# A decode block with a key and value cache: the load buffers moved by 192 bytes in SBUF

## The chip, the cores and the metric

The kernel runs on one core of a Trainium2 chip. The core has a matrix engine (TensorE, PE in the profile), a vector engine (VectorE, DVE), an activation engine (ScalarE, ACT), a general engine (GpSimd, POOL) and a sync engine (SyncE, SP) that issues transfers here. Transfers between the device memory and the on-chip memory (SBUF, 128 partitions) run on 16 transfer engines. SBUF is addressed by partition and by byte within the partition; this case is about the byte at which buffers begin. The metric is the device time of one execution in microseconds.

## The reference

The input `x` has 4 rows of 512. It is normalized to mean 0 and variance 1 over the 512 and goes into two branches, whose results are added to `x`:

```python
xn = layernorm(x)                                   # (4, 1, 512)
q  = (xn @ wq)                                      # 4 batches x 32 heads x 128
s  = einsum("bhqd,bhkd->bhqk", q, k_cache) * 128**-0.5   # over 4096 positions
o  = einsum("bhqk,bhkd->bhqd", softmax(s), v_cache)
out = x + o_flat @ wo + silu(xn @ w1) @ w2
```

`k_cache` and `v_cache` are 4 batches x 32 heads x 4096 positions x 128 floats each, 268 MB apiece; `wq` and `wo` are 8.4 MB each, `w1` and `w2` (512 x 1792 and back) 3.7 MB each. Everything is float32. There is one query per batch and head, so each element of the caches is used once.

## The kernel before

A tile of the cache holds four heads of one batch: 4 x 4096 positions x 128 floats, put on 128 partitions with 128 positions of 128 floats each. That is 65536 bytes a partition, contiguous in the device memory as well as in SBUF, and 8.389 MB in all. There are T = 32 such tiles of K and 32 of V, and the main loop (line 338) runs over them.

SBUF is given out by pools (lines 68 to 71), in this order: `const` for constants, `kpool` with two buffers of a tile, `vpool` with one, and `small` for short-lived tiles. So the size of all the tiles in `const` sets the byte at which the first buffer of `kpool` begins, and the following ones come right behind. A tile is asked for with a shape, a type and a name; nothing is executed by that.

All large transfers are issued by SyncE, in the order of the program: `load_tile` (line 76) asks for a buffer and issues one transfer, at line 80. The buffers also serve for other things: `w1` and `x` are loaded into parts of a K buffer (lines 84 to 91), `wq` into the V buffer (line 92), and at the end `wo` into the V buffer and `w2` into a K buffer, cut into pieces (lines 363 to 370). A transfer waits on SyncE until its buffer is free.

In step i of the loop:

- SyncE issues the K tile of step i + 1 and then, when the value matmuls of step i - 1 have let go of the single V buffer, the V tile of step i.
- `products` (line 265) multiplies K by the query on VectorE, 32 positions of each partition at a time, in place; the query comes from PSUM. GpSimd (line 269) adds the upper half of the 128 products to the lower half, for some of the positions, and VectorE sums what is left (`sums`, lines 280 and 281).
- `maxima` (lines 285 to 293) takes the maximum over four rows of partitions, `softmax` (line 299) exponentiates on ScalarE into `p_t`.
- `values` (line 310) multiplies `p_t` by V on TensorE: 32 instructions in the program, 64 matmuls in the trace, into the PSUM tile `o_ps`.
- `heads_out` (lines 323 to 331) sorts the four heads out and adds them into the PSUM tile `o_all`.

The last V tile goes into a K buffer (line 352). After the loop the heads are divided by their sums, transposed and multiplied by `wo` and most of `w2` (line 404), the rest of `w2` is added by `accumulate` (line 148), and the result goes out through `res` (lines 413 to 417).

Of the kernel before, what the change touches and what calls it, by code (L numbers as in the profile page):

```python
# [8 lines left out]
F32 = mybir.dt.float32  # L9
# [14 lines left out]
def kernel(  # L24
# [24 lines left out]
    P = nc.NUM_PARTITIONS  # L49
# [18 lines left out]
    const = ctx.enter_context(tc.tile_pool(name="const", bufs=1))  # L68
# [7 lines left out]
    def load_tile(pool, name, cache, i):  # L76
        t = pool.tile([P, R, Dh], F32, name=name)
        h, b = i // B * G, i % B
        src = cache[b, h : h + G].rearrange("h s d -> (h s) d")
        nc.sync.dma_start(t, src.rearrange("(p r) d -> p r d", p=P))  # L80
        return t
# [11 lines left out]
    nc.sync.dma_start(wq_t, wq.rearrange("(p c) n -> p c n", p=P))  # L93
    ks = {0: load_tile(kpool, "k_t", k_cache, 0)}

    ident = const.tile([P, P], F32, name="ident")
    make_identity(nc, ident)
    ones = const.tile([P, 1], F32, name="ones")
# [351 lines left out]
```

## Time and profile before

| | us |
|---|---|
| median of 3 runs | 1308.52 (1308.26 to 1309.41) |
| the profiled execution | 1307.8 |
| its span, first to last instruction | 1306.0 |
| VectorE busy | 973.8 (75%) |
| GpSimd busy | 510.9 (39%) |
| TensorE busy | 354.7 (27%) |
| ScalarE busy | 92.6 (7%) |
| read from the device memory | 561.00 MB, 430 GB/s over the span |

Times in the profile are microseconds unless marked ns, L12 is line 12 of the kernel, and "out<-in" names the tiles that an instruction writes and reads. A strip of 40 digits divides the span (or a stretch of it) into equal slices; a digit is the busy share in tenths. Rows of the transfer queues give the packets, their bytes, and the time that they took as a share of the time of 16 engines; the smallest packets carry a few bytes, the largest one partition of a load. In the rows by stretch, the pairs are busy time and number of instructions of TensorE, its weight loads, VectorE, ScalarE and GpSimd, and behind them come the granted clock of TensorE, the share of the transfer engines and the rate in GB/s. A row of waits reads: engine, what waited, what it waited for, then the total in us, how many times, and the longest.

### The profile page before, as it was taken

The page shows a single profiled execution, that of the slowest core. Times are in us where ns is not written, and L with a number is a line of the kernel's source. Part 1 is how long each engine was busy: PE and PEld are TensorE (multiplying, and loading weights), DVE is VectorE, ACT ScalarE, POOL GpSimd, SP SyncE. Part 2 cuts the span into 40 slices and gives each one's busy share as a digit, 9 for nine tenths or more (in the row PEclk, how much of TensorE's full clock was granted, in tenths as well). Part 3 has the DMA queues.
Part 4 walks back from the last instruction along what each step waited for, and adds up shares of the span by engine and source line. Part 5 has one row for each costly group of instructions (what it writes and reads, how often), then busy time and mean ns, then how long its engine had stood idle before and what let it go on. Part 6 is the DMA issues. An engine that isn't in the chain of part 4 may idle for free.

```text
span 1306.0 us, 6301 instructions
## 1 busy us (share of the span) xinstructions
PE 354.7 (27%) x2484; PEld 87.0 (7%) x2484; DVE 973.8 (75%) x540; ACT 92.6 (7%) x297; POOL 510.9 (39%) x142
## 2 busy tenths in 40 slices
PE   4221223221223321133322132322122232113237
PEld 1000000000000000000000000000000000000002
DVE  1499777887777797777797777788777789777770
ACT  1010000000000000000000000000000000000000
POOL 0255333444333444332444433344433344433340
PEclk9755666656666665666665566665566666566668
DMA  9999999999999999999999999999999999999997
GB/s 408 442 426 442 424 440 428 438 430 438 430 434 434 432 436 430 438 428 438 430 432 436 432 434 432 434 432 436 430 436 430 438 428 440 426 442 422 444 420 330
DMA packets 10437, 561.40 MB, mean 430 GB/s; under 512 B 1172, under 2 KB 1188, under 8 KB 1448
## 3 DMA queue, kind: packets, MB, share of 16 engines
q1 hardware_dynamic: 10392, 561.01, 99.4%
q8 instruction: 19, 0.31, 0.1%
q14 instruction: 10, 0.08, 0.0%
q10 hardware_dynamic: 16, 0.00, 0.0%
HBM read 561.00 MB, written 0.01 MB: 430 GB/s over the span
## 4 chain that ended last, share of the span: by engine, by line
DMA 70%; PE 22%; another core or an unknown queue 4%; DVE 2%; issue 2%; POOL 0%; ACT 0%; SPq 0%; POOLq 0%; ACTq 0%
DMA v_t<-in_A_v_cache_dram 61%; PE o_ps L310 20%; DMA k_t<-in_A_k_cache_dram 4%; DMA k_t<-in_A_v_cache_dram 3%; DMA v_t<-in_A_wq_dram 2%; DVE k_t L265 1%; PE q_ps L404 1%; PE sm L219 1%; DVE s L281 1%; POOL k_t L269 0%; DVE s L280 0%; PE acc L148 0%; PE sm L391 0%; PE q_ps L233 0%
## 5 line engine op out<-in xcount | busy, mean ns | idle before, releaser
L269 POOL TENSOR_TENSOR k_t<-k_t 128x2048 f32<-128x2048 f32 (+1 forms) x128 | 508.6, 3985 | 748.5 <-DVE k_t L265 748.5
L265 DVE TENSOR_TENSOR k_t<-k_t,q_ps 128x4096 f32<-128x4096 f32 x128 | 562.3, 4414 | 226.9 <-DMA k_t<-in_A_k_cache_dram 226.9
L310 PE MATMUL o_ps<-v_t,p_t 128*16 128x512 f32 x1984 | 285.2, 739 | 829.8 <-DMA v_t<-in_A_v_cache_dram 829.8
L281 DVE TENSOR_REDUCE s<-k_t 128x32 f32<-128x2048 f32 (+1 forms) x128 | 257.7, 2014 | 11.9 <-POOL k_t L269 11.9
L310 PEld LDWEIGHTS o_ps<-v_t,p_t 128*16 128x16 f32 x1984 | 66.5, 113 | 1030.1 <-issue 951.1
L323 ACT ACTIVATE o_sb<-o_ps 128x512 f32<-128x512 f32 x32 | 19.1, 597 | 1097.8 <-issue 1081.9
L280 DVE TENSOR_REDUCE s<-k_t 128x16 f32<-128x2048 f32 x32 | 72.8, 2276 | 0.0
L299 ACT ACTIVATE p_t<-s,nb 32x128 f32<-32x128 f32 x128 | 66.5, 519 | 17.4 <-DVE nb L293 14.0
L326 DVE TENSOR_TENSOR o_sb<-o_sb,own 128x512 f32<-128x512 f32 x32 | 21.7, 678 | 26.5 <-ACT o_sb L323 26.4
L331 PE MATMUL o_all<-o,w_t 128*32 128x128 f32 x64 | 15.7, 336 | 88.7 <-DVE o L330 88.7
L330 DVE TENSOR_REDUCE o<-o_sb 128x128 f32<-128x512 f32 x32 | 32.8, 1024 | 3.2
L299 ACT ACTIVATION_READ_ACCUMULATOR p_t<-s,nb 32x1 f32 x128 | 25.5, 199 | 0.0
L331 PEld LDWEIGHTS o_all<-o,w_t 128*32 128x32 f32 x64 | 4.9, 118 | 118.0 <-DVE o L330 118.0
L414 DVE COPY s<-acc 128x128 f32<-128x128 f32 x1 | 0.3, 292 | 14.8 <-PE acc L148 14.8
L310 PE MATMUL o_ps<-k_t,p_t 128*16 128x512 f32 x64 | 8.4, 684 | 6.5 <-DMA k_t<-in_A_v_cache_dram 6.5
L404 PE MATMUL q_ps<-v_t,ot 128*4 128x512 f32 x64 | 9.9, 788 | 0.4 <-DVE ot L396 0.4
L285 DVE TENSOR_REDUCE m_t<-s 128x1 f32<-128x128 f32 x32 | 9.1, 285 | 1.1
L208 DVE COPY ht_sb<-sm 128x64 f32<-128x64 f32 x1 | 0.2, 224 | 12.7 <-PE sm L201 12.7
L293 DVE STREAM_TRANSPOSE nb<-mb 128x32 f32<-128x32 f32 x32 | 6.8, 212 | 3.3
L219 PE MATMUL sm<-v_t,xpad 128*32 128x512 f32 x64 | 8.5, 690 | 1.3 <-DMA v_t<-in_A_wq_dram 1.3
L250 PE MATMUL q_ps<-q_h,ident 32*32 32x512 f32 x64 | 8.5, 599 | 0.8 <-DVE q_h L240 0.8
L229 DVE COPY o_sb<-sm 128x512 f32<-128x512 f32 x1 | 0.7, 692 | 9.5 <-PE sm L219 9.5
(74 smaller groups left out, 72.0 us busy)
## 6 DMA issues: line engine op xcount, KB each, us to landing
v_t<-in_A_wo_dram SPq DMA_DIRECT2D x2, 4096.0 KB
k_t<-in_B_w_dram SPq DMA_DIRECT2D x1, 3584.0 KB, 11.3
k_t<-in_B_w_dram SPq DMA_DIRECT2D x1, 1792.0 KB, 31.9
k_t<-in_B_w_dram SPq DMA_DIRECT2D x1, 1024.0 KB, 34.0
k_t<-in_A_k_cache_dram SPq DMA_DIRECT2D x32, 48.5
k_t<-in_B_w_dram SPq DMA_DIRECT2D x1, 512.0 KB, 34.8
v_t<-in_A_v_cache_dram SPq DMA_DIRECT2D x31, 29.3
k_t<-in_B_w_dram SPq DMA_DIRECT2D x1, 256.0 KB, 35.0
```

What stands on the lines that cost most here:

```text
L219: nc.tensor.matmul(qp[32 * j : 32 * j + 32, :], xpad[:, c, a : a + PH], wq_t[:, c, n * G * Dh : (n + 1) * G * Dh], start=(m == 0 and c == ...
L265: nc.vector.tensor_tensor(k[:, a:z, :], k[:, a:z, :], q[:, None, :].to_broadcast([P, STEP, Dh]), op=ALU.mult)
L269: nc.gpsimd.tensor_tensor(k[:, a:v, :half], k[:, a:v, :half], k[:, a:v, half:], op=ALU.add)
L280: nc.vector.tensor_reduce(s[:, v:z], k[:, v:z, :], axis=AX, op=ALU.add)
L281: nc.vector.tensor_reduce(s[:, a:v], k[:, a:v, :half], axis=AX, op=ALU.add)
L299: nc.scalar.activation(p_t[rows, :, g], s[rows, :], AF.Exp, bias=nb[rows, :1], scale=scale, accum_out=l_t[rows, i % B, i // B, g : g + 1],)
L310: last = nc.tensor.matmul(o[j : j + NR * G, :], p_t[:, rows, :].rearrange("p r g -> p (r g)"), v[:, rows, :].rearrange("p r d -> p (r d)") ...
L323: nc.scalar.activation(o_sb.rearrange("p r d -> p (r d)"), o_ps, AF.Copy)
L326: nc.vector.tensor_tensor(o_sb, o_sb, own[:, :, None].to_broadcast([P, NR, Dh]), op=ALU.mult)
L330: nc.vector.tensor_reduce(o_1, o_sb.rearrange("p r d -> p d r"), axis=AX, op=ALU.add)
L331: nc.tensor.matmul(o_all[:, b, :], w_t[:, W0 - h : W0 - h + H], o_1, start=False, stop=(i == T - 1))
L404: nc.tensor.matmul(part[j : j + B, :], a, w, start=(c < 4), stop=(c >= len(rows) - 4))
```

## The change

One tile is added to the pool `const`, after `xpad` and ahead of `ident`:

```diff
     ks = {0: load_tile(kpool, "k_t", k_cache, 0)}
 
+
+    const.tile([P, 48], F32, name="fill")
     ident = const.tile([P, P], F32, name="ident")
```

It has 48 floats, 192 bytes, on each partition. No instruction writes or reads it. The tiles of `const` behind it and all the buffers of `kpool`, `vpool` and `small` begin 192 bytes further on; the buffers of the loads begin at byte 26880, which is 105 x 256. All other lines are the same, and those behind the added ones have numbers larger by 2.

## The prediction

> **What bounds the kernel now.** I read the two strips of the page for the transfers first, then the chain of waits, then single steps of the loop, then the packets of the transfer queue.
>
> ```profile
> span 1306.0 us, 6301 instructions
> DVE  1499777887777797777797777788777789777770
> DMA  9999999999999999999999999999999999999997
> DMA packets 10437, 561.40 MB, mean 430 GB/s; under 512 B 1172, under 2 KB 1188, under 8 KB 1448
> ```
>
> The transfer engines are busy in every slice but the last, while VectorE, the busiest compute engine, sits at seven or eight tenths. The chain of waits in order of time shows how one step of the loop hangs on them (start, duration, what):
>
> ```profile
> 1060.39 9.48 PE o_ps L310 x64
> 1069.90 29.06 DMA v_t<-in_A_v_cache_dram
> 1098.96 0.14 issue
> 1099.09 8.91 PE o_ps L310 x64
> 1108.02 29.64 DMA v_t<-in_A_v_cache_dram
> 1137.66 0.14 issue
> 1137.79 10.04 PE o_ps L310 x64
> ```
>
> The value matmuls of two neighbouring steps start 1099.09 - 1060.39 = 38.70 us and 1137.79 - 1099.09 = 38.70 us apart. The step is therefore not set by matmuls, whose bursts vary from 8.91 to 10.04 us. The busy time in those two steps, by engine, with the share of the transfer engines and their rate at the end of each row:
>
> ```profile
> 1060.39:1099.09 38.70, 10.84 (x74) 2.49 (x75) 30.20 (x17) 2.68 (x9) 15.89 (x5) 0.63 1.00 432
> 1099.09:1137.79 38.70, 9.28 (x66) 2.26 (x67) 30.41 (x18) 2.68 (x9) 15.88 (x5) 0.63 1.00 434
> ```
>
> VectorE (third pair) works 30.2 to 30.4 us of 38.70, TensorE 9 to 11, GpSimd 15.9; the transfer share is 1.00. A step loads one K tile and one V tile, 2 x 8.389 MB. So the kernel is a transfer stream at 16.78 MB / 38.70 us = 433.5 GB/s, with compute beside it. Who waits tells how much cover the compute has:
>
> ```profile
> PE o_ps L310 <- DMA v_t<-in_A_v_cache_dram: 829.8, 31, 46.8
> DVE k_t L265 <- DMA k_t<-in_A_k_cache_dram: 226.9, 30, 9.2
> ```
>
> TensorE waits for every V tile. VectorE waits 226.9 / 30 = 7.6 us for a K tile. In the chain above a V load needs 29.06 to 29.64 us from issue to landing, of which its own share is half a step, 19.35; so it stands about 9.8 us behind a K load that is still moving, and the transfer engines are never without work.
>
> **The change, part by part.** It adds a tile and no instruction: no compute, no transfer, no wait, no step moved past a queue. It does three things.
>
> *The place of everything after it.* 48 floats are 192 bytes. The load buffers move from 26880 - 192 = 26688 bytes (104 x 256 + 64) to 26880 (105 x 256). A buffer is 65536 bytes a partition, also a multiple of 256, so all three had the same offset of 64 and all three lose it. Every constant after `xpad`, and the small tiles behind the buffers, move by the same 192, so the buffers, `p_t` and `q_h` keep their distances; `xpad` alone stays and is read only in the start-up.
>
> *The compute.* Whether an engine reads the shifted buffers at another speed no row tells. The present times on both K buffers are, as minimum, median and maximum:
>
> ```profile
> L265 DVE TENSOR_TENSOR k_t<-k_t,q_ps x128: 4394/4412/4422, 51.9 to 1253.2; 128x4096 f32<-128x4096 f32 x128
> ```
>
> VectorE can lose 38.70 - 30.3 = 8.4 us per step before it sets the pace, 28% of its work. TensorE can lose the 9.8 us by which the V load is issued ahead of its turn; that would double its burst. I cost the compute at 0 under this cover. If the cover went, the products of L265 would be late next.
>
> *The packets.* This is the only term that could matter. In the stretch of 26 steps, and in two short stretches at the end that hold nothing but small packets, the transfer queues show (packets, MB, share of 16 engines):
>
> ```profile
> DMA packets 7514, 436.83 MB, mean 433 GB/s; under 512 B 832, under 2 KB 832, under 8 KB 832
> q1 hardware_dynamic: 7493, 436.54, 100.1%
> ...
> DMA packets 2, 0.00 MB, mean 0 GB/s; under 512 B 2, under 2 KB 2, under 8 KB 2
> q1 hardware_dynamic: 2, 0.00, 0.2%
> ...
> DMA packets 32, 0.01 MB, mean 2 GB/s; under 512 B 16, under 2 KB 32, under 8 KB 32
> q10 hardware_dynamic: 16, 0.00, 0.5%
> q1 hardware_dynamic: 16, 0.00, 0.5%
> ```
>
> The first pair of rows is from 129.34 to 1137.79 us: 7493 - 832 = 6661 large packets carry 436.54 MB, 65536 bytes each, one for each partition of a load. Sixteen engines share the 256 of a step, so an engine moves 16 of them in 38.70 us, 2.419 us each. The second pair covers 0.5 us with two of the smallest packets: 0.2% of 16 x 0.5 us is 16 ns, 8 ns each, though they carry almost nothing. The third covers 3.5 us: 1.0% of 16 x 3.5 is 0.56 us; without 16 of the smallest at 8 ns it leaves 0.43 us for the 16 packets of the output, which are 8 KB in all, 512 bytes each: 27 ns each. At the stream's rate 512 bytes take 2419 x 512 / 65536 = 18.9 ns. So a packet has a fixed cost of about 8 ns; with the shares rounded to a tenth it is 4 to 12.
>
> How many packets count? The end follows the last V tile, here in a K buffer:
>
> ```profile
> 1274.14 8.39 PE L310 MATMUL o_ps<-k_t,p_t 128*16 128x512 f32 x64 [6.50 <-DMA k_t<-in_A_v_cache_dram]
> 1288.08 9.93 PE L404 MATMUL q_ps<-v_t,ot 128*4 128x512 f32 x64 [0.38 <-DVE ot L396]
> 1302.78 0.29 DVE L414 COPY s<-acc 128x128 f32<-128x128 f32 x1 [14.76 <-PE acc L148]
> ```
>
> From its landing to the last copy 28.6 us pass in matmuls and small operations that no alignment shortens, with the weights arriving beside them. Up to that landing an engine has moved 8 packets for each of 64 K and V loads, for `wq` and for `w1`: 66 x 8 = 528. The sum is therefore 528 times the change in one packet, and every ns per packet is 0.53 us. The queue being full, all of it reaches the end.
>
> What is that change? At the one end, the whole fixed cost is due to the offset and goes: -8 ns, -4.2 us (by the 12 ns, -6.3). At the other end, nothing excludes a loss; I bound it by the same cost coming twice, +4.2 us. Between them I go by the row that is nearest, the smallest packets: they write no load buffer and pay 8 ns all the same. The cost is then that of a packet, not of where a buffer begins. I take 0 ns. The sum is 0 on a span of 1306.0 us. The profiled execution took 1307.8 us in all, 0.7 below the median of 1308.52; with no change the forecast is that median, 1308.5.
>
> The Trainium skill, page "DMA: Bandwidth & Descriptors", section "Where 436 GB/s comes from", gives a ceiling of 435.2 GB/s. The trace's 433.5 agrees in being just below; by the page, an estimate, a step at the ceiling would be 38.55 us, and 33 such steps would save 5.0 us, so it too leaves no room for a large gain.
>
> **The rivals.**
>
> *A. The 64 bytes below the offset are moved and thrown away.* Each packet would then carry 65600 bytes' worth of time for 65536: 2419 x 64 / 65536 = 2.4 ns, times 528 = 1.25 us. Without it the time is 1307.3. For it speaks that 2.4 ns fits inside the 8 ns; against it, that the offset is on the written side while the caches are read from rows of 65536 bytes. That rule is in the same page of the Trainium skill, section "How a descriptor splits into AXI transactions": a transaction must start at a 256-byte boundary, and the bytes ahead of the start are fetched without use. The page tells it of reading, and no run here shows it yet for writing.
>
> *B. The fixed cost is the offset's.* A packet that begins and ends inside a 256-byte block may pay for two broken pieces instead of none. Then all 8 ns go: 1308.5 - 4.2 = 1304.3. For it: nothing in this kernel is loaded to another offset, so no row separates the two. Against it: the smallest packets' 8 ns, and the output's 8 ns, whose destination is not a load buffer.
>
> *C. Slower: packets that begin on the boundary get longer.* The place is the write of each 64 KB packet into the buffers; for instance, engines that now start on the same boundary could hold each other up. If the fixed cost doubles, 528 x 8 ns = 4.2 us, 1312.7. It decides from 0.2%, 2.6 us, that is 5 ns a packet. Against it: the buffers keep their distances to each other and all shared one offset before, too. For it: only that no row excludes it.
>
> *D. The change doesn't do what it says.* The tile is never written or read; if it got no room, nothing would move and the time would stay 1308.5. The time can't tell this from the forecast.
>
> **How the numbers follow.** The three times shown spread over 1308.26 to 1309.41, 0.09%, so I take 0.2%, 2.6 us, as what a measurement can tell from no change. Chances: forecast 0.40, A 0.25, B 0.17, C 0.15, D 0.03. The forecast, A and D lie within 0.2%: 0.68. B is faster, 0.17. C is slower, 0.15. The likeliest case's own range is 1306.9 to 1309.6 (A to the highest time shown, each with 0.03% of spread). The range for 8 in 10 takes in B at 1304.3 with some spread, and the smaller half of C: 1303.7 to 1311.0.
>
> **What would show each step.** If I am right, the steps of the loop stay at 38.70 us between value matmuls and the last V tile lands 1274 us after the start. By A they are 16 x 2.4 ns = 0.04 us shorter, by B 0.13 us (38.57), by C 0.13 us longer; the last landing moves by 1.25, 4.2 or -4.2 us. L265 should stay at 4.41 us and the bursts of L310 at 8.4 to 10 us; another time there would show that compute feels the offset, within its cover. The stretch from the last landing to the last copy should stay at 28.6 us. The prediction is wrong if a packet's time depends on the buffer's place by more than 5 ns, or if the offset changes what a transfer does for every piece of 256 bytes, of which a packet has 256: a single ns on each would be 256 ns a packet and 135 us in all. The stream's steadiness near one rate is my reason to think that this isn't so.

## The result and the profile after

The changed kernel takes 1305.28 us (median; 1304.97 to 1306.11) beside 1308.10 us (1307.72 to 1309.59) for the kernel before: the ratio is 0.9978, with a 95% interval of 0.9970 to 0.9986, so it is 1.8 to 3.9 us faster. That is 2.8 us, just beyond the 2.6 us that the prediction took as the bound of no change, and 3.2 us below the forecast of 1308.5. One execution of a later run, the one at offset 128, took 1670.35 us, far from the other 11, and is left out of its time and ratio. The profiled execution took 1305.64 us, 1303.9 of it span. Lines of the kernel behind the new tile have numbers larger by 2: L310 is L312, L265 is L267.

The strips of the page say what they said before:

```profile
span 1303.9 us, 6301 instructions
DVE  1499777887777797777797777788777779777770
DMA  9999999999999999999999999999999999999997
DMA packets 10437, 561.40 MB, mean 431 GB/s; under 512 B 1172, under 2 KB 1188, under 8 KB 1448
```

The same 10437 packets with the same bytes pass in 2.1 us less. The chain of waits over the same two steps, and the busy time in them:

```profile
1058.23 8.85 PE o_ps L312 x64
1067.09 29.63 DMA v_t<-in_A_v_cache_dram
1096.86 10.01 PE o_ps L312 x64
1106.88 28.49 DMA v_t<-in_A_v_cache_dram
1135.51 9.46 PE o_ps L312 x64
```

```profile
1058.23:1096.86 38.63, 10.20 (x75) 2.42 (x75) 30.09 (x17) 2.68 (x9) 15.91 (x5) 0.63 1.00 435
1096.86:1135.51 38.65, 10.50 (x67) 2.43 (x68) 30.55 (x18) 2.69 (x9) 15.90 (x5) 0.59 1.00 434
```

The two steps are 38.63 and 38.65 us long, not 38.70: 0.06 us less on average. An engine moves 16 large packets in a step, so a packet takes about 0.06 / 16 = 4 ns less. Two steps give the size only roughly: over 26 steps the mean fell from (1137.79 - 129.34) / 26 = 38.79 us to (1135.51 - 129.13) / 26 = 38.71, 0.08 us or 5 ns a packet. The transfer share is still 1.00; the same engines are full, with less to do. VectorE's product is as long as it was, and the waits for K and V hardly move:

```profile
L267 DVE TENSOR_TENSOR k_t<-k_t,q_ps x128: 4395/4413/4422, 51.5 to 1250.8; 128x4096 f32<-128x4096 f32 x128
...
PE o_ps L312 <- DMA v_t<-in_A_v_cache_dram: 826.2, 31, 46.5
...
DVE k_t L267 <- DMA k_t<-in_A_k_cache_dram: 224.6, 30, 9.0
```

The end, in order of time:

```profile
1271.72 9.57 PE L312 MATMUL o_ps<-k_t,p_t 128*16 128x512 f32 x64 [7.21 <-DMA k_t<-in_A_v_cache_dram]
...
1300.62 0.29 DVE L416 COPY s<-acc 128x128 f32<-128x128 f32 x1 [12.90 <-PE acc L150]
```

The last V tile lands at 1271.72 us, 2.42 us earlier than at 1274.14. From there to the last copy it is 28.90 us, 0.26 more than before; the burst of matmuls at the landing took 9.57 us here and 8.39 there, which is within what such bursts vary by. So the gain is made in the stream, and the tail passes it on.

### The profile page after: what moved, and what is told of

It reads as the page before. It is cut to its first block, busy times and chain, and to the rows that moved or that the text cites. A ratio compares the mean times of both kernels' runs of the same rounds, so it can differ in the third digit from the quotient of the medians.

```text
span 1303.9 us, 6301 instructions
## 1 busy us (share of the span) xinstructions
PE 356.0 (27%) x2484; PEld 88.1 (7%) x2484; DVE 973.8 (75%) x540; ACT 92.7 (7%) x297; POOL 511.2 (39%) x142
## 2 busy tenths in 40 slices
DMA packets 10437, 561.40 MB, mean 431 GB/s; under 512 B 1172, under 2 KB 1188, under 8 KB 1448
## 4 chain that ended last, share of the span: by engine, by line
DMA 71%; PE 23%; another core or an unknown queue 4%; issue 2%; DVE 0%; ACT 0%; SPq 0%; ACTq 0%
DMA v_t<-in_A_v_cache_dram 65%; PE o_ps L312 21%; DMA k_t<-in_A_v_cache_dram 3%; DMA v_t<-in_A_wq_dram 2%; PE q_ps L406 1%; PE sm L221 1%; PE sm L393 0%; PE acc L150 0%; PE q_ps L235 0%; PE q_ps L252 0%; DVE o L332 0%; DVE o_sb L328 0%; DVE q_h L242 0%; DVE o_sb L231 0%
## 5 line engine op out<-in xcount | busy, mean ns | idle before, releaser
L267 DVE TENSOR_TENSOR k_t<-k_t,q_ps 128x4096 f32<-128x4096 f32 x128 | 562.3, 4414 | 224.6 <-DMA k_t<-in_A_k_cache_dram 224.6
L312 PE MATMUL o_ps<-v_t,p_t 128*16 128x512 f32 x1984 | 286.1, 741 | 826.2 <-DMA v_t<-in_A_v_cache_dram 826.2
L312 PEld LDWEIGHTS o_ps<-v_t,p_t 128*16 128x16 f32 x1984 | 66.6, 113 | 1027.3 <-issue 948.3
L312 PE MATMUL o_ps<-k_t,p_t 128*16 128x512 f32 x64 | 9.6, 765 | 7.2 <-DMA k_t<-in_A_v_cache_dram 7.2
```

Source lines behind the costliest of these rows:

```text
L267: nc.vector.tensor_tensor(k[:, a:z, :], k[:, a:z, :], q[:, None, :].to_broadcast([P, STEP, Dh]), op=ALU.mult)
L312: last = nc.tensor.matmul(o[j : j + NR * G, :], p_t[:, rows, :].rearrange("p r g -> p (r g)"), v[:, rows, :].rearrange("p r d -> p (r d)") ...
```

## The experiments

By now the theory was that the offset of the buffers, their distance behind a multiple of 256 bytes, costs something in each packet. It had to be told from others: that some other tile's place matters, that the cost grows with the offset (the prediction's A), and that each packet pays a fixed price at any offset (its B). All kernels are the kernel before with the edits shown; their ratios are to the kernel before, run on the same chip.

**Moving everything by 256 bytes.**

```diff
+    const.tile([P, 64], F32, name="fill")
     ident = const.tile([P, P], F32, name="ident")
```

> The fill tile has 64 floats, 256 bytes: everything moves further than in the change, but the load buffers keep their offset of 64 bytes from a multiple of 256. If the offset is the cause, the time is that of the kernel before (1308.1 us, ratio 1.000) and a step of the loop stays at 38.70 us. If moving things in itself or another address is the cause, the time falls by about 2.8 us, to 1305.3.

Measured: 1308.02 us, ratio 0.9998 (0.9990 to 1.0007). The value matmuls of three steps start at 1060.52, 1099.22 and 1137.92 us, 38.70 us apart as expected. Other addresses with the same offset of 64 bytes give the time of the kernel before; moving alone does nothing that these runs can tell.

**Only the load buffers.**

```diff
     ot = const.tile([P, H, B], F32, name="ot")
+    const.tile([P, 48], F32, name="fill")
```

> The same 48 floats, but as the last tile of the constants: the load buffers and the small tiles move by 192 bytes to the multiple of 256, the constants (ident, p_t, q_h and the others) stay where they were. If the load buffers' offset is the cause, all of the gain is there: 1305.3 us, ratio 0.998, step of 38.62 us. If it is the constants that an engine reads, the time stays at 1308.1.

Measured: 1305.32 us, ratio 0.9980 (0.9972 to 0.9989): the whole gain, with the constants where they were before. What counts is the place of the buffers (or of the small tiles behind them, which move too; the next pairs, in which the packets are multiplied, rule these out).

**Other offsets.** The same tile with 16, 32 and 56 floats puts the buffers 128, 192 and 32 bytes behind a multiple of 256:

```diff
+    const.tile([P, 16], F32, name="fill")
     ident = const.tile([P, P], F32, name="ident")
```

> 16 floats: the load buffers begin 128 bytes behind a multiple of 256. If the bytes below the offset are moved and thrown away, the cost grows with the offset and is twice that of 64 bytes: some 2.8 us slower than the kernel before, 1310.9 (1309.4 by the strict price of 1.25 us per 64 bytes). If a broken piece at each end of a packet is the cause, any offset costs the same: 1308.1. If only multiples of 128 matter: 1305.3.

> 32 floats: the load buffers begin 192 bytes behind a multiple of 256. Bytes thrown away: three times the cost of 64 bytes, 5.6 us slower than the kernel before, 1313.7 (1310.6 by the strict price). A broken piece at each end: 1308.1 as before.

> 56 floats: the load buffers begin 32 bytes behind a multiple of 256. Bytes thrown away: half of the cost of 64 bytes, 1.4 us faster than the kernel before, 1306.7 us. A broken piece at each end: no change, 1308.1.

Measured, with 64 and 0 beside them (32 ran on another chip than 64, 128 and 192; there the kernel before took 1308.29 us, and 1308.05 with those):

| offset, bytes | us | ratio to before (95%) |
|---|---|---|
| 0 (the change) | 1305.28 | 0.9978 (0.9970 to 0.9986) |
| 32 | 1308.75 | 1.0003 (0.9994 to 1.0012) |
| 64 (moved by 256) | 1308.02 | 0.9998 (0.9990 to 1.0007) |
| 128 | 1307.80 | 0.9998 (0.9989 to 1.0006) |
| 192 | 1308.10 | 0.9999 (0.9990 to 1.0008) |

The bursts of value matmuls in the chains of waits, two following ones each at offset 128, then 192, then 32, then with the buffers alone moved to 0:

```profile
1099.09 8.41 PE o_ps L311 x64
1137.79 9.54 PE o_ps L311 x64
```

```profile
1099.17 9.05 PE o_ps L311 x64
1137.88 8.46 PE o_ps L311 x64
```

```profile
1099.41 8.87 PE o_ps L311 x64
1138.12 9.99 PE o_ps L311 x64
```

```profile
1097.23 8.70 PE o_ps L310 x64
1135.87 9.86 PE o_ps L310 x64
```

The steps are 38.70, 38.71 and 38.71 us at the three offsets and 38.64 at 0. Bytes thrown away in proportion to the offset would have put 192 bytes 2.5 us above the kernel before by the strict price; it is not there. A has fallen: 64, 128 and 192 bytes cost the same within the intervals. Whether 32 costs a little more stayed open here.

**Only V.** The tile of 48 floats goes first into the pool of V, so that K keeps the offset of 64:

```diff
+    vpool.tile([P, 48], F32, name="fill")
     wq_t = vpool.tile([P, R, Dh], F32, name="v_t")...
```

> 48 floats as the first tile of the pool of V: only the V buffer moves to a multiple of 256, both K buffers keep the offset of 64 bytes. If the cost lies in the packets, V's 33 of the 66 loads lose it: half of the gain, 1.4 us, 1306.7 us, and a step of 38.66 us. If it is only the K buffers, which VectorE and GpSimd read and write, 1308.1; if only V, 1305.3.

Measured: 1306.45 us, ratio 0.9987 (0.9978 to 0.9996), 1.8 us below the kernel before on that chip; the interval is 0.5 to 2.9 us. It takes in half of the gain and excludes no gain; the whole gain it does not exclude. The value matmuls of two following steps:

```profile
1059.11 9.64 PE o_ps L311 x64
1097.77 9.09 PE o_ps L311 x64
```

That step is the 38.66 us that was expected of half the packets. Over 26 steps, from 129.16 to 1136.41 us, the mean is 38.74, between the 38.79 of the kernel before and the 38.71 of the change. The small tiles behind the V buffer move here too, but the constants and the K buffers do not. V's buffer, whose cache tiles only TensorE reads, gives a part without K's, so the cost isn't tied to VectorE's and GpSimd's work on K.

**Eight times as many packets.** Each load of a cache tile becomes eight transfers of 8192 bytes a partition, at offset 64 and, with the change's tile, at offset 0:

```diff
-        nc.sync.dma_start(t, src.rearrange("(p r) d -> p r d", p=P))
+        src = src.rearrange("(p r) d -> p r d", p=P)
+        for a in range(0, R, R // 8):
+            nc.sync.dma_start(t[:, a : a + R // 8, :], src[:, a : a + R // 8, :])
```

> Each load of a K or V tile is cut into eight transfers, so that the packets are of 8192 bytes and there are eight times as many, with the old offset of 64 bytes. Compared with its twin at offset 0 (the next kernel), a cost per packet shows eight times: 8 x 2.8 = 22 us between the two. A cost per byte shows as before, 2.8 us. Against the kernel before, the fixed cost of seven more packets in eight gives some 512 x 7 x 5 ns = 18 us, and the last tile can be begun earlier.

> The same eight transfers per load, with the change's fill tile: the buffers begin on a multiple of 256. If the cost of the offset is one per packet, this is 22 us faster than its twin at offset 64; if it goes with the bytes, 2.8 us faster.

Measured: 1343.82 us at offset 64, ratio 1.0273 (1.0259 to 1.0287), and 1326.45 at offset 0, ratio 1.0140 (1.0126 to 1.0154). The difference is 17.4 us: more than six times the 2.8 of the single transfers, less than the 22 expected. Against the kernel before, the version at offset 64 is 35.5 us slower, about twice the 18 expected. That sum took 5 ns for each of 512 x 7 = 3584 further packets; the 9.5 ns found below make 34 us of it. The chain of waits now consists of loads; two following ones at offset 64, then at 0:

```profile
435.57 19.87 DMA k_t<-in_A_k_cache_dram
455.45 19.86 DMA v_t<-in_A_v_cache_dram
```

```profile
430.62 19.61 DMA k_t<-in_A_k_cache_dram
450.25 19.61 DMA v_t<-in_A_v_cache_dram
```

From load to load it is 19.88 us and 19.63. An engine moves 64 packets for a load, so the offset costs 0.25 / 64 = 3.9 ns in a packet of 8192 bytes, as much as in one of 65536. It is a cost per packet and not per byte. The transfer queue of SyncE is still full in both, by its row in the stretch from 129 to 1137 us, offset 64 first (a share above 100% means that recorded packets overlap):

```profile
q1 hardware_dynamic: 58308, 424.58, 101.2%
```

```profile
q1 hardware_dynamic: 59072, 430.20, 101.0%
```

The pair also shows what a packet costs at offset 0. A load takes half of 38.64, 19.32 us, in 8 packets and 19.63 in 64: 0.31 / 56 = 5.5 ns for each further packet, with its share of the seven further completions. At offset 64 it is (19.88 - 19.35) / 56 = 9.5 ns.

**The offset on the read side.** The two kernels with eight transfers, but each tile of the caches, the last one excepted, is read 16 floats further on:

```diff
-        src = cache[b, h : h + G].rearrange("h s d -> (h s) d")
+        o, n = (b * H + h) * S * Dh, G * S * Dh
+        o += 16 if i < T - 1 else 0
+        src = cache.rearrange("b h s d -> (b h s d)")[o : o + n].rearrange("(x d) -> x d", d=Dh)
```

> Eight transfers per load into buffers at offset 0, but every tile of the caches except the last of each is read 64 bytes (16 floats) further on in the device memory, so its values are the neighbours' and the output is not the reference's. If only the written side pays for an offset, the time is that of the eight transfers at offset 0, 1326.5 us. If an offset on the read side breaks a packet too, it is that at offset 64, 1343.8, or by the page's rule on fetched bytes (two beats of 1.18 ns a packet) about 1336.

> As the one before, read 64 bytes further on (values not the reference's), but written to the buffers at the old offset of 64 bytes, so both sides have the same offset. If the cost comes from the two sides standing differently within 256 bytes, it is gone: 1326.5 us, and the one before costs 1343.8. If the written side pays alone: 1343.8. If each side pays for itself and the costs add: 1361.

Measured: 1327.12 us into offset 0, ratio 1.0142 (1.0129 to 1.0156), and 1344.13 into offset 64, ratio 1.0274 (1.0260 to 1.0288). Two following loads each:

```profile
430.49 19.61 DMA k_t<-in_A_k_cache_dram
450.12 19.61 DMA v_t<-in_A_v_cache_dram
```

```profile
435.54 19.86 DMA k_t<-in_A_k_cache_dram
455.42 19.86 DMA v_t<-in_A_v_cache_dram
```

The steps from load to load are 19.63 and 19.88, the same as without the shift. Moving the read side by 64 bytes changes nothing; the written side pays alone. Since 64 bytes were added to the source, it can't have been on a multiple of 256 in both kernels.

The Trainium skill, page "DMA: Bandwidth & Descriptors", section "How a descriptor splits into AXI transactions", says that a read that starts off a 256-byte boundary fetches the bytes below it too. For this shift that would be 64 bytes more in each packet, two of the section's beats of 32 bytes. At the stream's rate they take 2419 x 64 / 65536 = 2.36 ns, so 62 shifted loads of 64 packets would be some 9.4 us longer by this estimate. The trace shows no such time: 19.63 us a load with and without. Whether the bytes are fetched without delaying the load no run here shows.

**A larger boundary, and the offset of 32 again.**

```diff
+    const.tile([P, 496], F32, name="fill")
     ident = const.tile([P, P], F32, name="ident")
```

> One transfer per load, with a fill tile of 496 floats, so that the buffers begin at byte 28672, a multiple of 4096 (the change's 26880 is a multiple of 256 and not of 512). If 256 bytes are all that counts, the time is that of the change, 1305.3 us. If a boundary of 512 or more gives something further, it is less; a further packet cost of 2 ns would show as 1 us.

> Eight transfers per load, buffers at an offset of 32 bytes. If any offset costs one fixed amount per packet, this is the twin at offset 64, 1343.8 us. If the cost goes with the offset, 1335. If an offset that is no multiple of 64 costs another nanosecond per packet (one transfer per load at 32 bytes came out 0.5 us above the kernel before, within the uncertainty), it is about 4 us more: 1348.

Measured: at a multiple of 4096 1305.53 us, ratio 0.9980 (0.9971 to 0.9989), the time of the change. A boundary beyond 256 bytes gives nothing that these runs can tell. The byte at which the buffers begin stands in no view of the trace, but the moves and the times alone point to 256: moves of 192 and 1984 bytes, which are 7 x 256 apart, gain, and moves of 64, 128, 224 and 256 bytes do not. No other power of two fits all six as a period. The kernel with eight transfers at offset 32 (the edits of the eight transfers with a fill tile of 56 floats) takes 1349.01 us, ratio 1.0309 (1.0295 to 1.0323). Its loads:

```profile
437.06 19.93 DMA k_t<-in_A_k_cache_dram
457.01 19.93 DMA v_t<-in_A_v_cache_dram
```

They follow in 19.95 us: 0.32 / 64 = 5.0 ns a packet above offset 0. So the offset of 32 bytes costs about one nanosecond more than that of 64; other offsets below 64 were not run. With one transfer per load that is 528 ns in all, the size of the 0.5 us that could not be told from nothing above.

## Why the prediction was right and where it was wrong

*What bounds the kernel.* Right. The stream sets the step before and after, and when a packet got shorter, the step and the end got shorter with it.

*The compute at 0.* Right: L267 takes 4.413 us where L265 took 4.412, and with the constants in their old place the gain is the same.

*528 packets, each nanosecond worth 0.53 us.* Right. 528 times the 3.9 ns measured with eight transfers is 2.1 us, which is what the spans of the two profiled executions differ by, and lies in the interval of the timed runs, 1.8 to 3.9. For eight transfers per load it is 64 x 64 + 16 = 4112 packets: 16 us by this price, 17.4 measured, which is 4.2 ns a packet.

*A fixed cost of about 8 ns per packet, 4 to 12.* Right in size: 9.5 ns at the old offset, with the completions' share in it.

*The change in one packet taken as 0.* This is the step that failed. The argument was that the smallest packets pay 8 ns although they write no load buffer, so that the cost belongs to the packet. The runs show that the fixed cost has two parts: some 5.5 ns that stay at offset 0, completions included, and 4 to 5 ns that the offset of 64 adds. A small packet that pays a similar sum proves nothing on how the sum of a large one is made up. The forecast of no change was therefore wrong in its mechanism, and the result lies below the 1306.9 that bounded its likeliest case, between A's 1307.3 and B's 1304.3. The range of 1303.7 to 1311.0 holds it only because it was drawn to reach B, not by the reasoning that gave 0.

*Rival A.* Fallen: the cost isn't proportional to the offset, and reading 64 bytes further on adds none.

*Rival B.* Right in what the time depends on: a packet that doesn't begin (and so doesn't end) on the boundary pays a price that is the same at 64, 128 and 192 bytes. That the price is one of broken pieces no run shows. It was priced too high, with the whole 8 ns instead of 4 to 5: the step of 38.57 us that it foresaw came out as 38.63 to 38.65, and the landing moved by 2.4 us and not 4.2.

*Rivals C and D.* Neither happened. No packet got longer, and the tile moves the buffers.

What stays open: by what mechanism the packet gets longer, and whether the 4 ns are paid at its beginning, at its end, or in two halves. The large packets all have a length that is a multiple of 256, so an offset always moves both ends off the boundary, and no run separated them. The exact size stays open too: 3.9 ns from the loads with eight transfers and 5 ns from the mean of 26 steps make 2.1 to 2.6 us of 528 packets, beside 2.8 between the medians; the interval takes all of these in.

## What to carry to other kernels

In a kernel that a stream of transfers bounds, count the packets of one transfer engine on the path and price an alignment by the packet: here a destination off a multiple of 256 bytes in SBUF cost 4 to 5 ns in each, 0.2% with packets of 64 KB and 1.3% with packets of 8 KB (17.4 of 1326.45 us). It costs one unused tile to try, and the control is a tile of 256 bytes, which moves everything and keeps the offset. A row that shows a cost elsewhere doesn't tell how much of the same cost here is avoidable; where only the sum is known, keep both ends and let the range reach them.

## What the runs showed that was not expected

- The size of the offset hardly matters: 64, 128 and 192 bytes give 1308.02, 1307.80 and 1308.10 us. Only 32 bytes, with 5.0 ns a packet against 3.9, stands out.
- Moving the read side by 64 bytes doesn't matter: 19.63 us a load with the source 64 bytes on, 19.63 without.
- A multiple of 256 that is none of 512 (26880) is as good as a multiple of 4096 (28672): 1305.28 and 1305.53 us.
